# Sliding-window attention with sinks, followed by a maxout FFN: the order of the opening's instructions, chunks 0 to 3, written anew

## The chip, the cores and the metric

One Trainium2 chip, one of its cores. The metric is device time in microseconds (us), the median of the runs shown. The core has five engines that run their own instruction queues in order: TensorE (PE: matrix products, results to PSUM), VectorE (DVE), ScalarE (ACT), GpSimd (POOL) and SyncE (SP, which issues most transfers).

## What is computed

```python
scores = scale * np.matmul(q, k.transpose(0, 1, 3, 2))     # q, k, v: 4 x 8 x 768 x 64
keep = is_sink | in_window                                 # 4 sink keys, window of 128
scores = np.where(keep, scores, -1000000000.0)
scores = scores - np.max(scores, axis=-1, keepdims=True)
a = np.exp(scores)
a = a / (np.sum(a, axis=-1, keepdims=True) + 1e-09)
attn_out = np.matmul(a, v)
x = attn_out.transpose(0, 2, 1, 3).reshape(B * S, H * D)   # 3072 x 512
h = np.maximum(np.maximum(x @ w1, x @ w2), x @ w3)         # 3072 x 768
out = h @ w_out                                            # 3072 x 512
```

## The kernel before

**Tiling.** The 3072 tokens are 12 chunks of 256, three to a batch. A chunk's query rows see their own keys, the last 128 keys of the chunk before, and the four sinks of the batch (chunks 0, 3, 6 and 9 begin a batch and need neither). The eight heads are four pairs p. For each chunk c the kernel

- loads q, k and v (`load`, on SP's queue; a `gate` is a tiny write by GpSimd that the load has to wait for), casts them to bf16 (`cast_qk(c, w, g, engine)`, half g holding pairs 2g and 2g+1; `cast_v(c, n, i, engine)`, four quarters), and turns q and k with TensorE transposes and a copy out of PSUM (`turn`, L138 to L149; `turn2`), or by a transposing transfer (`turn_dma`);
- computes a pair's scores into two PSUM banks (`score`, L331). In chunks 0 and 1 the mask of some pairs is first put into the bank by a product (`premask`, L311); others are multiplied by a 0/1 mask after the exponential (`mask`, VectorE, L406). The masks are built by GpSimd and VectorE (`masks`, `factors`, `masks2`);
- takes the exponential on ScalarE, two halves to a pair (`expo`, L398), the sinks apart (`sink_k`, `sink_score`, `sink_v`);
- multiplies by the values, with a column of ones for the row sums (`av_open` takes four banks and adds the sinks' share; `av(c, p)`, L471), divides (`norm`, VectorE, L481 and L484) and turns the result to `xT` (`xpose`, L496 and L498, two halves; from chunk 3 on `xpose_dma`, one transfer);
- projects: `ffn_h(c, fp, wi)` is eight products with columns 256 fp to 256 fp + 255 of matrix wi (0, 1, 2 for w1, w2, w3) into one bank (L524), and `ffn_max` takes the bank into `h`: a copy for wi = 0 (L536, ScalarE unless told otherwise), a maximum for the others (L540, VectorE). With `then=False`, `av` and `ffn_h` leave `norm` and `ffn_max` to be written at another place. `ffn_y(c, t)` is half of the output product (L553, six products of 512 columns).

**The weights** come by GpSimd's queue in pieces (`load_w(wi, first column, last column)`, L292; `load_wo`).

**Order.** Nothing schedules: under `manual_schedule` each engine takes its instructions in the order in which the program's lines are written. The opening, chunks 0 to 3 with the attention of chunk 4, is one long list written out by hand, with the work of several chunks interleaved. From `for i in range(4, NCH)` a loop's body has one fixed order.

**PSUM.** Eight banks are handed out from a list, the one released longest ago first (`bank` and `give`). A write into a bank waits for what read it last, so the place of an `expo`, a `norm` or an `ffn_max` in the list sets when a later product can start.

`warm(n)` runs n products of zeros whose result nobody reads.

Of the kernel before, what the change touches and what calls it, by code (L numbers as in the profile page):

```python
# [999 lines left out]
```

## Time and profile before

| | us |
|---|---|
| median of 3 runs | 175.49 |
| lowest, highest | 175.13, 176.15 |
| the profiled execution's span, first to last instruction | 173.5 |
| TensorE busy in it | 167.7 |
| VectorE, GpSimd, ScalarE busy | 125.1, 110.1, 88.8 |

The profile is that of one execution. A timeline row gives an instruction's (or a run of equal instructions') start and length in us from the span's start, the engine, the line, what it writes and reads, and in brackets how long the engine stood idle before it and what ended that. A queue's name (POOLq, SPq) stands for the issuing of a transfer. Two equal instructions in a row overlap a little, so a run of them is shorter than the sum of their lengths.

### The profile page before, as it was taken

The numbers are of one execution on the slowest core, as the hardware profiler recorded it, in microseconds if no ns is written. First come the engines' busy times: TensorE is split into PE (matmuls) and PEld (weight loads), VectorE is DVE, ScalarE is ACT, GpSimd is POOL, SyncE is SP. The second block draws the span as 40 slices with busy tenths as digits, with TensorE's granted clock in tenths as the row PEclk, the third lists the DMA queues.
The fourth block names the chain that finished last, engine by engine and source line by source line (L and its number), as shares of the span: only waits on it lengthen the run. The fifth ranks groups of instructions, "written<-read, shape, count | busy, mean of one in ns | idle before, by whom it ended". The sixth has DMA issues, their size and how long they took to land.

```text
span 173.5 us, 5418 instructions
## 1 busy us (share of the span) xinstructions
PE 167.7 (97%) x2225; PEld 129.2 (74%) x2225; DVE 125.1 (72%) x262; ACT 88.8 (51%) x183; POOL 110.1 (63%) x193
## 2 busy tenths in 40 slices
PE   7979999999999999999999999999999999999992
PEld 2546889857695697797797797797897896896871
DVE  3187856696697985986877977877778876776361
ACT  4598554587944615817726717627636516510210
POOL 7389507445399999999999999999998700000000
PEclk9999999999999999999999999999999999999999
DMA  4999999999996999988999969969999119017303
GB/s 134 300 289 198 216 217 252 219 274 290 292 210 118 250 264 180 252 188 220 264 186 247 264 165 254 257 163 238 257 176 274 32 34 376 21 35 272 121 2 121
DMA packets 71545, 35.22 MB, mean 203 GB/s; under 512 B 27488, under 2 KB 69984, under 8 KB 71520
## 3 DMA queue, kind: packets, MB, share of 16 engines
q1 hardware_dynamic: 65824, 31.60, 79.0%
q0 software_dynamic: 5552, 3.15, 12.8%
q8 instruction: 17, 0.28, 0.7%
q10 hardware_dynamic: 144, 0.13, 0.2%
q14 instruction: 8, 0.07, 0.1%
HBM read 25.17 MB, written 6.29 MB: 181 GB/s over the span
## 4 chain that ended last, share of the span: by engine, by line
PE 93%; DVE 3%; ACT 1%; issue 0%
PE h_ps L524 55%; PE y_ps L577 11%; PE y_ps L553 7%; PE o L471 7%; PE st L357 3%; PE warm L203 3%; PE st L331 3%; PE pt L138 2%; ACT e_sb L398 1%; PE o L453 1%; DVE x_sb L484 1%; PE sk L423 1%; PE y_ps L599 1%; DVE vb L123 1%; PE xt L496 1%; PE st L311 0%
## 5 line engine op out<-in xcount | busy, mean ns | idle before, releaser
L524 PE MATMUL h_ps<-xT,w 128*128 128x256 bf16 x864 | 101.2, 273 | 0.1
L524 PEld LDWEIGHTS <-w 128*128 128x128 bf16 x864 | 81.9, 98 | 9.9 <-issue 0.3
L540 DVE TENSOR_TENSOR h_sb<-h_sb,h_ps 128x512 bf16<-128x512 bf16 (+1 forms) x74 | 49.3, 671 | 20.0 <-PE h_ps L524 16.0
L536 ACT CAST h_sb<-h_ps 128x512 bf16<-128x512 f32 x35 | 20.5, 585 | 52.2 <-PE h_ps L524 52.2
L129 POOL CAST vb<-v_raw 32x512 bf16<-32x512 f32 x48 | 36.7, 764 | 2.8 <-DMA v_raw<-in_v_dram 0.6
L90 POOL CAST k_bf<-k_raw 32x512 bf16<-32x512 f32 x48 | 29.5, 614 | 2.2
L398 ACT ACTIVATE e_sb<-st 128x512 bf16<-128x512 f32 (+1 forms) x48 | 23.1, 588 | 0.7 <-PE st L331 0.7
L484 DVE TENSOR_TENSOR x_sb<-o,rc 128x256 bf16<-128x256 f32 x48 | 20.4, 424 | 1.6
L577 PE MATMUL y_ps<-wo,h_sb 64*64 64x512 bf16 (+1 forms) x312 | 21.1, 377 | 0.0
L471 PE MATMUL o<-vb,e_sb 128*128 128x65 bf16 x352 | 16.8, 193 | 0.4 <-ACT e_sb L398 0.4
L471 PEld LDWEIGHTS <-e_sb 128*128 128x128 bf16 x352 | 14.6, 97 | 2.8 <-issue 0.8
L123 POOL CAST vb<-v_raw 64x512 bf16<-64x512 f32 x18 | 12.4, 691 | 5.8 <-DMA v_raw<-in_v_dram 5.2
L389 DVE TENSOR_TENSOR e_sb<-e_part,msk 128x1024 bf16<-128x1024 bf16 x16 | 13.5, 865 | 3.1 <-ACT e_part L374 3.0
L406 DVE TENSOR_TENSOR e_sb<-e_sb,msk 128x1024 bf16<-128x1024 bf16 (+1 forms) x18 | 13.3, 756 | 2.1 <-ACT e_sb L398 2.0
L577 PEld LDWEIGHTS <-h_sb 64*64 64x64 bf16 (+1 forms) x312 | 9.9, 106 | 5.0
L374 ACT ACTIVATE e_part<-st 128x384 bf16<-128x384 f32 x32 | 13.1, 496 | 0.5 <-PE st L357 0.5
L553 PE MATMUL y_ps<-wo,h_sb 128*128 128x512 bf16 x54 | 13.0, 380 | 0.0
L481 DVE RECIPROCAL rc<-o 128x4 f32<-128x4 f32 x48 | 8.3, 174 | 3.5 <-PE o L471 3.4
L118 POOL CAST k_bf<-k_raw 128x512 bf16<-128x512 f32 x6 | 3.8, 647 | 9.6 <-DMA k_raw<-in_k_dram 9.4
L553 PEld LDWEIGHTS <-h_sb 128*128 128x128 bf16 x54 | 4.8, 97 | 5.6 <-DVE h_sb L540 0.9
L118 ACT CAST q_bf<-q_raw 128x512 bf16<-128x512 f32 x13 | 7.6, 621 | 2.0 <-DMA q_raw<-in_q_dram 1.9
L427 ACT ACTIVATE e_sink<-sk 128x256 bf16<-128x256 f32 x8 | 3.1, 389 | 10.0 <-PE sk L423 10.0
(90 smaller groups left out, 144.2 us busy)
## 6 DMA issues: line engine op xcount, KB each, us to landing
k_raw<-in_k_dram SPq DMA_DIRECT2D x11, 512.0 KB, 5.7
v_raw<-in_v_dram SPq DMA_DIRECT2D x11, 512.0 KB, 5.8
q_raw<-in_q_dram SPq DMA_DIRECT2D x10, 512.0 KB, 6.5
out_dram<-y_sb SPq DMA_DIRECT2D x9, 512.0 KB, 3.1
w<-in_moe_w_dram POOLq DMA_DIRECT2D x9, 256.0 KB, 6.6
q_raw<-in_q_dram SPq DMA_DIRECT2D x4, 256.0 KB, 7.7
out_dram<-y_sb SPq DMA_DIRECT2D x1, 1024.0 KB, 5.2
wo<-in_moe_w_out_dram POOLq DMA_DIRECT2D x2, 384.0 KB, 7.4
```

The lines of the kernel that those rows point to most:

```text
L90: f(bfs[ci, "k"][x:x + 32, :, n], raws[ci, "k"][y:y + 32, :, i].rearrange("q (p a) d -> q p a d", a=2))
L123: eng.tensor_copy(vb[ci % RING][64 * i:64 * i + 64, n, :, 0:D], raws[ci, "v"][64 * n:64 * n + 64, :, i])
L129: eng.tensor_copy(vb[ci % RING][x:x + 32, n, :, 0:D], raws[ci, "v"][y:y + 32, :, i])
L389: nc.vector.tensor_mul(x.rearrange("q a (t s) c -> q (a t) s c", t=2), y, msk2)
L398: nc.scalar.activation(e[:, a, lo:], st[a][:, lo:], AF.Exp, scale=scale)
L471: nc.tensor.matmul(o[:, t, a], lhsT=e[:, a, s], rhs=vb[cv % RING][:, n, 2 * p + a], start=first, stop=True, skip_group_check=True)
L484: nc.vector.tensor_mul(xs[ci][:, p], o[:, :, :, 0:D], rc.unsqueeze(3).to_broadcast([128, 2, 2, D]))
L524: nc.tensor.matmul(hp[:, f].rearrange("q (i t r) -> q i t r", i=2, r=x.shape[3]), lhsT=w_sb[wi][:, ds, c0:c0 + 128], rhs=x, start=(ds == 0 ...
L536: (nc.scalar.copy if eng is nc.scalar else eng.tensor_copy)(dst, hp)
L540: nc.vector.tensor_max(dst[:, x], dst[:, x], hp[:, x])
L553: nc.tensor.matmul(yp, lhsT=hs[ci][:, fb, t * 128:(t + 1) * 128], rhs=wo[:, fb], start=(fb == 0), stop=(fb == FB - 1))
L577: nc.tensor.matmul(yps[ci][t][c:c + cols], lhsT=hs[ci][hp, fb, x:x + cols], rhs=wo[hp, fb], start=(turn == 0 and fb == 0), stop=(turn == 1 ...
```

## The change

Only the list of the opening is rewritten. The helper functions and the loop stay, and the computation is the same; one warm product of twelve goes.

- *Chunk 0:* `masks()` is written ahead of the casts, the mask products of two pairs ahead of the first turn, K is cast before Q, four of the warm products go behind the scores, and V's gate stands behind the masks on GpSimd.
- *Weights:* the first two pieces of w1 are issued before chunk 1's K cast; the last piece of w3 behind the cast of chunk 2's K.
- *Chunks 0 to 4:* every division and every maximum is now written apart from its products, most of them later. First copies (wi = 0) of some projections go from ScalarE to VectorE, three of the four V casts of chunk 5 from GpSimd to VectorE, the Q casts of chunk 4 from VectorE to ScalarE; `ffn_y(2, 1)`'s copy goes to ScalarE, `ffn_y(1, 1)`'s to VectorE.

The core of the difference:

```diff
         load(0, 'q', part=1, parts=2)
-        warm(8)
+        warm(7)
+        masks()
         load(0, 'k')
+        cast_qk(0, 'k', 1, nc.vector)
         load(0, 'q', part=0, parts=2)
         load(0, 'v', part=0, parts=2, gate=pool_gate)
-        cast_qk(0, 'q', 1, nc.scalar)
         load(0, 'v', part=1, parts=2)
-        masks()
         sink_init()
+        cast_qk(0, 'k', 0, nc.scalar)
+        premask(0, (2,))
+        cast_qk(0, 'q', 1, nc.gpsimd)
+        premask(0, (1,))
+        turn(0, 'q', 1, nc.vector)
+        turn(0, 'k', 1, nc.vector)
         factors(msk, addm)
-        turn(0, 'q', 1, nc.scalar)
+        cast_qk(0, 'q', 0, nc.vector)
+        turn(0, 'k', 0, nc.vector)
+        premask(0, (3,))
+        load(1, 'k')
+        cast_v(0, 1, 0, nc.gpsimd)
+        score(0, (2,))
+        expo(0, 2)
+        turn(0, 'q', 0, nc.vector)
+        score(0, (3,))
+        expo(0, 3)
+        cast_v(0, 0, 0, nc.vector)
+        premask(0, (0,))
+        load_w(0, 512, 768)
+        score(0, (0,))
+        load(1, 'q')
+        expo(0, 0)
+        score(0, (1,))
+        load(1, 'v')
+        cast_v(0, 1, 1, nc.vector)
         warm(4)
-        premask(0, (2,))
-        cast_qk(0, 'k', 0, nc.scalar)
-        cast_qk(0, 'k', 1, nc.vector)
-        turn(0, 'k', 1, nc.vector)
-        load(1, 'k')
-        turn(0, 'k', 0, nc.scalar)
-        cast_qk(0, 'q', 0, nc.gpsimd)
-        premask(0, (3,))
-        score(0, (2,))
-        score(0, (3,))
-        turn(0, 'q', 0, nc.vector)
-        premask(0, (0,))
-        load(1, 'q')
-        expo(0, 2)
-        cast_v(0, 1, 0, nc.gpsimd)
-        cast_v(0, 0, 0, nc.vector)
-        cast_v(0, 1, 1, nc.vector)
+        expo(0, 1)
         cast_v(0, 0, 1, nc.vector)
-        load_w(0, 512, 768)
-        load(1, 'v')
-        score(0, (0,))
-        expo(0, 3)
+        av_open(0)
+        av(0, 3, then=False)
+        norm(0, 3)
+        premask(1, (1,))
+        av(0, 2, then=False)
+        norm(0, 2)
+        premask(1, (0,))
+        av(0, 0, then=False)
+        load_w(0, 256, 512)
+        norm(0, 0)
+        cast_qk(1, 'k', 1, nc.scalar)
+        turn(1, 'k', 1, nc.vector)
+        av(0, 1, then=False)
+        norm(0, 1)
         cast_qk(1, 'k', 0, nc.gpsimd)
-        premask(0, (1,))
-        score(0, (1,))
-        expo(0, 0)
-        expo(0, 1)
-        load_w(0, 256, 512)
-        av_open(0)
-        av(0, 2)
-        av(0, 3)
-        turn2(1, 'k', 0, nc.vector)
...
         score(1, (0,))
+        expo(1, 0)
+        load_w(1, 256, 512)
         score(1, (1,))
-        expo(1, 0)
+        xpose(0, 1, nc.vector)
+        score(1, (3,))
+        expo(1, 3)
+        cast_v(1, 1, 1, nc.gpsimd)
+        sink_score(1)
+        load_w(1, 0, 256)
+        ffn_h(0, 2, 0, then=False)
+        ffn_max(0, 2, 0, 1, nc.vector)
+        score(1, (2,))
+        av_open(1)
+        cast_v(1, 1, 0, nc.gpsimd)
+        av(1, 0, then=False)
+        load(2, 'k', part=0, parts=2, gate=after(0, 300))
         expo(1, 1)
-        load_w(1, 256, 512)
-        cast_v(1, 1, 1, nc.gpsimd)
-        xpose(0, 1, nc.vector)
-        cast_v(1, 0, 1, nc.gpsimd)
-        load_w(1, 0, 256)
-        score(1, (3,))
-        sink_score(1)
-        load(2, 'k', part=0, parts=2, gate=after(0, 300))
+        av(1, 1, then=False)
+        ffn_h(0, 1, 0, then=False)
         load(2, 'k', part=1, parts=2)
-        sink_v(0)
-        expo(1, 3)
-        ffn_h(0, 2, 0, 1, nc.vector)
-        score(1, (2,))
-        load(2, 'q', part=1, parts=2)
         load(2, 'q', part=0, parts=2, gate=pool_gate)
+        expo(1, 2)
         load_w(2, 0, 256)
-        expo(1, 2)
+        mask(1, 3)
+        factors(msk0[0], addm0)
+        av(1, 3, then=False)
         load_w(2, 256, 512)
-        load_w(2, 512, 768)
-        av_open(1)
-        av(1, 0, then=False)
-        av(1, 1, then=False)
-        mask(1, 3)
-        ffn_h(0, 1, 0)
         norm(1, 0)
         mask(1, 2)
-        av(1, 3, then=False)
-        ffn_h(0, 0, 0)
+        ffn_h(0, 0, 0, then=False)
+        load(2, 'q', part=1, parts=2)
+        norm(1, 3)
+        av(1, 2, then=False)
+        norm(1, 1)
         load(2, 'v', gate=after(0, 300))
-        norm(1, 1)
-        av(1, 2, then=False)
-        norm(1, 3)
+        norm(1, 2)
...
+        ffn_h(1, 1, 0, then=False)
+        load_w(2, 512, 768)
+        ffn_h(0, 0, 1, then=False)
         load_wo()
-        factors(msk0[0], addm0)
-        ffn_h(1, 0, 1)
-        turn(2, 'k', 0, nc.vector)
+        ffn_max(0, 0, 0, 1, nc.vector)
         cast_v(2, 1, 0, nc.gpsimd)
+        ffn_max(1, 0, 0)
+        ffn_h(1, 1, 1, then=False)
+        ffn_max(1, 1, 0)
+        turn(2, 'k', 1, nc.scalar)
+        cast_qk(2, 'q', 0, nc.vector)
+        ffn_max(1, 1, 1)
+        ffn_max(1, 0, 1)
+        turn(2, 'q', 0, nc.scalar)
...
+        ffn_max(2, 0, 0, 1, nc.vector)
+        ffn_h(2, 1, 0, then=False)
+        ffn_h(2, 0, 1, then=False)
+        mask(3, 0)
+        ffn_max(2, 0, 2)
+        ffn_max(2, 1, 0)
+        mask(3, 3)
         score(3, (2,))
-        ffn_h(2, 0, 2)
-        mask(3, 0)
-        mask(3, 3)
-        ffn_h(2, 1, 0)
-        ffn_h(2, 0, 1)
         expo(3, 2)
         av_open(3)
+        ffn_max(2, 0, 1)
+        av(3, 1, then=False)
+        av(3, 0, then=False)
+        ffn_h(2, 2, 0, then=False)
+        sink_k(1)
+        ffn_h(2, 1, 1, then=False)
+        norm(3, 1)
+        av(3, 3, then=False)
+        cast_v(4, 1, 0, nc.gpsimd)
         mask(3, 2)
-        av(3, 0)
-        av(3, 1)
-        ffn_h(2, 1, 1, then=False)
-        av(3, 3)
-        ffn_h(2, 2, 0)
-        av(3, 2)
+        av(3, 2, then=False)
+        load(6, 'q')
+        ffn_h(2, 2, 1, then=False)
+        norm(3, 0)
+        cast_qk(5, 'k', 0, nc.gpsimd)
+        ffn_max(2, 2, 0)
+        norm(3, 3)
+        norm(3, 2)
+        cast_qk(5, 'k', 1, nc.scalar)
+        xpose_dma(3)
...
         cast_qk(5, 'q', 1, nc.gpsimd)
-        load(6, 'k')
-        turn_dma(5, 'q')
-        load(6, 'v')
-        masks2()
-        cast_v(5, 0, 0, nc.gpsimd)
-        cast_v(5, 0, 1, nc.gpsimd)
-        cast_v(5, 1, 0, nc.gpsimd)
-        cast_v(5, 1, 1, nc.gpsimd)
...
+        cast_qk(5, 'q', 0, nc.scalar)
+        expo(4, 3)
+        mask(4, 3)
+        load(6, 'k')
+        ffn_h(3, 1, 0, then=False)
+        cast_v(5, 1, 1, nc.vector)
+        ffn_h(3, 0, 0, then=False)
+        expo(4, 2)
+        mask(4, 2)
+        cast_v(5, 0, 0, nc.vector)
         mask(4, 1)
-        expo(4, 2)
-        ffn_y(2, 1, nc.vector)
-        mask(4, 2)
-        expo(4, 3)
-        ffn_h(3, 0, 0)
-        mask(4, 3)
-        ffn_h(3, 0, 1)
+        load(6, 'v')
+        ffn_h(3, 0, 1, then=False)
         av_open(4)
-        av(4, 0)
-        ffn_h(3, 0, 2)
-        av(4, 1)
-        ffn_h(3, 1, 0)
-        av(4, 2)
-        ffn_h(3, 1, 1)
-        av(4, 3)
+        ffn_max(3, 0, 0)
+        ffn_max(3, 0, 1)
+        ffn_h(3, 2, 1, then=False)
+        ffn_h(3, 1, 2, then=False)
+        cast_v(5, 0, 1, nc.vector)
+        av(4, 3, then=False)
+        norm(4, 3)
```

What this makes of three queues follows; the names in the rows carry buffer numbers, which differ between the two programs.

GpSimd's queue, from the V cast of chunk 0 (`vb0`) to the sinks of K; `w0` and `w1` are the matrices w1 and w2. Before:

```order
L123 CAST vb0_77<-v_raw_125 64x8x64
L292 DMA w0_107<-in_moe_w1_dram 128x4x256
L118 CAST k_bf_232<-k_raw_181 128x2x2x2x64
L292 DMA w0_107<-in_moe_w1_dram 128x4x256
L118 CAST q_bf_287<-q_raw_214 128x2x2x2x64
L292 DMA w0_107<-in_moe_w1_dram 128x4x256
L283 COPY ks0_81<-kT0_69 64x4x4 x2
```

And now:

```order
L123 CAST vb0_77<-v_raw_145 64x8x64
L292 DMA w0_107<-in_moe_w1_dram 128x4x256 x2
L118 CAST k_bf_285<-k_raw_190 128x2x2x2x64
L292 DMA w0_107<-in_moe_w1_dram 128x4x256
L118 CAST q_bf_310<-q_raw_224 128x2x2x2x64
L283 COPY ks0_81<-kT0_69 64x4x4 x2
L292 DMA w1_108<-in_moe_w2_dram 128x4x256 x2
```

Two transfers of w1 now stand ahead of chunk 1's K cast, and all three ahead of its Q cast; before, casts and transfers took turns.

ScalarE's queue, the exponentials of chunk 1. Before, `e_sb_343`, `350`, `373` and `416` are pairs 0, 1, 3 and 2:

```order
L398 ACTIVATE e_sb_343<-st_306 128x512
L398 ACTIVATE e_sb_343<-st_307 128x512
L398 ACTIVATE e_sb_350<-st_317 128x512
L398 ACTIVATE e_sb_350<-st_318 128x512
L427 ACTIVATE e_sink_379<-sk_374 128x256
L398 ACTIVATE e_sb_373<-st_365 128x512
L398 ACTIVATE e_sb_373<-st_366 128x512
L398 ACTIVATE e_sb_416<-st_408 128x512
L398 ACTIVATE e_sb_416<-st_409 128x512
```

Now `e_sb_352`, `377`, `362` and `408` are pairs 0, 3, 1 and 2:

```order
L398 ACTIVATE e_sb_352<-st_271 128x512
L398 ACTIVATE e_sb_352<-st_272 128x512
L398 ACTIVATE e_sb_377<-st_369 128x512
L398 ACTIVATE e_sb_377<-st_370 128x512
L427 ACTIVATE e_sink_386<-sk_381 128x256
L398 ACTIVATE e_sb_362<-st_258 128x512
L398 ACTIVATE e_sb_362<-st_259 128x512
L398 ACTIVATE e_sb_408<-st_400 128x512
L398 ACTIVATE e_sb_408<-st_401 128x512
```

Pair 3 and the sinks now come ahead of pair 1.

VectorE's queue in chunk 3: L406 are the masks of its four pairs, L540 and L536 the maxima and a first copy of chunk 2's projections, L481 and L484 divisions. Before, with pairs 1, 0, 3, 2:

```order
L406 TENSOR_TENSOR e_sb_929<-e_sb_929,msk0_0_101 128x2x384
L123 CAST vb3_80<-v_raw_732 64x8x64
L540 TENSOR_TENSOR h_sb_945<-h_sb_945,h_ps_979 128x512
L406 TENSOR_TENSOR e_sb_940<-e_sb_940,msk0_0_101 128x2x384
L406 TENSOR_TENSOR e_sb_964<-e_sb_964,msk0_0_101 128x2x384
L540 TENSOR_TENSOR h_sb_945<-h_sb_945,h_ps_1001 128x512
L406 TENSOR_TENSOR e_sb_978<-e_sb_978,msk0_0_101 128x2x384
L481 RECIPROCAL rc_1024<-o_1013 128x4
L484 TENSOR_TENSOR x_sb_1026<-o_1013,rc_1024 128x256
L481 RECIPROCAL rc_1034<-o_1014 128x4
L484 TENSOR_TENSOR x_sb_1026<-o_1014,rc_1034 128x256
```

Now, in the same order of the pairs except that the mask of pair 2, the last L406, comes later:

```order
L406 TENSOR_TENSOR e_sb_947<-e_sb_947,msk0_0_101 128x2x384
L536 CAST h_sb_950<-h_ps_960 128x512
L406 TENSOR_TENSOR e_sb_930<-e_sb_930,msk0_0_101 128x2x384
L540 TENSOR_TENSOR h_sb_950<-h_sb_950,h_ps_951 128x512
L406 TENSOR_TENSOR e_sb_940<-e_sb_940,msk0_0_101 128x2x384
L540 TENSOR_TENSOR h_sb_950<-h_sb_950,h_ps_989 128x512
L481 RECIPROCAL rc_1048<-o_1012 128x4
L484 TENSOR_TENSOR x_sb_1050<-o_1012,rc_1048 128x256
L406 TENSOR_TENSOR e_sb_1008<-e_sb_1008,msk0_0_101 128x2x384
L481 RECIPROCAL rc_1077<-o_1011 128x4
L484 TENSOR_TENSOR x_sb_1050<-o_1011,rc_1077 128x256
L481 RECIPROCAL rc_1083<-o_1014 128x4
```

The four masks are drawn apart; the one of pair 2 now stands behind three maxima or copies and pair 1's division.

More of the change, by code (lines that the diff above doesn't have):

```diff
@@ new lines @@
+        ffn_h(0, 0, 2, then=False)
+        ffn_max(1, 1, 2)
+        ffn_max(0, 0, 2)
+        ffn_h(0, 1, 2, then=False)
+        ffn_max(0, 1, 2)
+        cast_qk(2, 'q', 1, nc.scalar)
+        turn(2, 'q', 1, nc.scalar)
+        ffn_max(1, 2, 1)
+        ffn_h(1, 0, 2, then=False)
+        ffn_max(1, 0, 2)
+        score(2, (0,))
+        score(2, (3,))
+        expo(2, 0)
+        load(3, 'k')
+        score(2, (1,))
+        expo(2, 1)
+        sink_score(2)
+        mask(2, 0)
+        ffn_h(1, 2, 2, then=False)
@@ L801 @@
-        av(2, 2)
-        ffn_y(1, 0)
-        turn(3, 'k', 1, nc.scalar)
-        turn(3, 'k', 0, nc.scalar)
+        load(4, 'q', gate=after(0, 300))
+        score(2, (2,))
+        expo(2, 2)
+        load(4, 'k', gate=after(0))
+        ffn_y(0, 0)
+        cast_v(2, 0, 0, nc.vector)
+        mask(2, 3)
+        cast_qk(3, 'k', 1, nc.scalar)
+        mask(2, 1)
+        av_open(2)
+        mask(2, 2)
+        av(2, 0, then=False)
+        av(2, 3, then=False)
+        load(4, 'v')
+        ffn_y(0, 1)
@@ new lines @@
+        norm(2, 3)
+        cast_qk(3, 'q', 1, nc.vector)
+        cast_qk(3, 'q', 0, nc.gpsimd)
+        load(5, 'k', gate=after(0, 300))
+        cast_qk(3, 'k', 0, nc.vector)
+        av(2, 1, then=False)
+        load(5, 'q')
+        norm(2, 0)
+        ffn_y(1, 0)
+        av(2, 2, then=False)
+        turn(3, 'q', 1, nc.scalar)
+        turn(3, 'k', 0, nc.scalar)
+        cast_v(3, 0, 0, nc.gpsimd)
+        norm(2, 1)
+        norm(2, 2)
+        turn(3, 'k', 1, nc.vector)
+        turn(3, 'q', 0, nc.scalar)
@@ L805 @@
         xpose(2, 0, nc.scalar)
+        cast_qk(4, 'q', 1, nc.scalar)
         xpose(2, 1, nc.vector)
[L807 to L819 removed]
@@ new lines @@
+        cast_qk(4, 'k', 0, nc.gpsimd)
+        score(3, (3,))
+        score(3, (1,))
+        expo(3, 1)
+        ffn_h(2, 0, 2, then=False)
+        ffn_h(2, 0, 0, then=False)
+        cast_qk(4, 'k', 1, nc.vector)
+        turn_dma(4, 'k')
+        expo(3, 3)
+        expo(3, 0)
+        mask(3, 1)
+        cast_v(4, 1, 1, nc.gpsimd)
+        cast_v(3, 0, 1, nc.gpsimd)
+        ffn_max(2, 0, 0, 1, nc.vector)
+        ffn_h(2, 1, 0, then=False)
+        ffn_h(2, 0, 1, then=False)
+        mask(3, 0)
```

168 lines of the change are left out of this document (66 added, 102 removed).

## The prediction

> **What bounds the kernel now.** I read the page's engine shares and its chain first, then the windows by stage and TensorE's waits, and last the timelines of the first 70 us.
>
> ```profile
> PE 167.7 (97%) x2225; PEld 129.2 (74%) x2225; DVE 125.1 (72%) x262; ACT 88.8 (51%) x183; POOL 110.1 (63%) x193
> ...
> PE 93%; DVE 3%; ACT 1%; issue 0%
> ...
> 44.26:53.94 9.68, 9.68 (x114) 8.14 (x113) 8.39 (x19) 5.44 (x12) 7.06 (x13) 1.00 1.04 212
> 53.94:67.42 13.48, 13.48 (x162) 9.88 (x162) 10.79 (x22) 6.20 (x12) 12.62 (x27) 1.00 1.16 226
> 67.42:173.50 106.08, 102.72 (x1490) 82.01 (x1489) 77.17 (x148) 48.33 (x103) 65.14 (x97) 1.00 0.79 184
> ```
>
> TensorE is 97% busy, and the chain that ended last runs 93% on it. The window columns are length, then PE, PE loads, VectorE, ScalarE and GpSimd busy. From 15.88 us (the first projection) to 67.42 us (the loop's first instruction, the sink scores of chunk 5) TensorE has no idle time. The loop's own order is not edited. So the change is worth what it moves the loop's start, 67.42, as long as what the loop needs is there by then.
>
> ```profile
> PE pt L138 <- ACT k_bf L118: 0.3, 1, 0.3
> ...
> 1.26 3.60 PE L203 MATMUL warm<-wz 128*128 128x512 bf16 x8 [1.26 <-DVE wz L192]
> 5.08 1.67 PE L203 MATMUL warm<-wz 128*128 128x512 bf16 x4
> 7.81 0.50 PE L331 MATMUL st<-qT,kT 64*128 64x256 bf16 x8
> 10.64 0.53 PE L471 MATMUL o<-vb,e_sb 128*128 128x65 bf16 x12 [0.44 <-ACT e_sb L398]
> 15.88 1.03 PE L524 MATMUL h_ps<-xT,w 128*128 128x256 bf16 x8
> 21.70 5.40 PE L524 MATMUL h_ps<-xT,w 128*128 128x256 bf16 x48
> 36.34 2.76 PE L553 MATMUL y_ps<-wo,h_sb 128*128 128x512 bf16 x12
> 44.26 0.51 PE L331 MATMUL st<-qT,kT 64*128 64x256 bf16 x8
> 53.94 0.25 PE L437 MATMUL sv<-vb,sel 128*32 128x65 bf16 x8
> 67.42 0.29 PE L423 MATMUL sk<-qT,ks 128*32 128x256 bf16 x4
> ```
>
> These rows (start, length) give milestones at which old and new order have done the same set of TensorE work: 15.88 (first projection), 21.70 (chunk 1 attended and transposed), 36.34 (first output product), 44.26 (scores of chunk 3), 53.94 (sinks before chunk 4), 67.42. The 48 products in 5.40 give a projection's eight: 0.9, with no gap 0.87. TensorE's idle that the rows show after 7 us is some 1 us (0.28 and 0.44 the largest), so a gain has a low ceiling; a loss has none.
>
> **The change part by part.** The work is the same but for one warm matmul. I walk each queue by hand in its new order, with durations from rows, and compare at the milestones; a change in a bank's wait is read from the rule that the eight PSUM banks are reused in order of release.
>
> *Opening, to the first projection.*
>
> ```profile
> 5.78 0.43 DVE L118 CAST k_bf<-k_raw 128x512 bf16<-128x512 f32 x1 [1.91 <-DMA k_raw<-in_k_dram]
> 7.33 0.42 DVE L149 COPY kT<-pt 128x512 bf16<-128x512 bf16 x1 [1.13 <-PE pt L138]
> 8.19 3.17 ACT L398 ACTIVATE e_sb<-st 128x384 bf16<-128x384 f32 x8
> 9.03 1.47 DVE L123 CAST vb<-v_raw 64x512 bf16<-64x512 f32 x3
> 8.61 0.61 POOL L123 CAST vb<-v_raw 64x512 bf16<-64x512 f32 x1 [1.29 <-DMA v_raw<-in_v_dram]
> 9.17 1.11 POOL L292 DMA_DIRECT2D w<-in_moe_w_dram  x1
> 10.95 0.75 POOL L292 DMA_DIRECT2D w<-in_moe_w_dram  x1
> 12.12 0.61 POOL L118 CAST q_bf<-q_raw 128x512 bf16<-128x512 f32 x1 [0.43 <-DMA q_raw<-in_q_dram]
> ```
>
> The mask products of two pairs now fill the wait for K, and four warm matmuls go behind the scores. K's cast ends at 6.21 either way; the transposes follow at once, and the copy of kT ends at 7.15 instead of 7.75, so the first score starts at 7.2 instead of 7.81 and the eight exponentials (0.396 each) end 0.6 earlier, at 10.8. But the values need V's casts. V lands at 8.6 as before (its issue is gated some 0.5 later, behind the masks, in a stream that has earlier loads to finish); the three casts on VectorE now start on landing and end at 10.1, so the first values start at 10.15, not 10.64. Then GpSimd: two weight issues (1.11 and 0.75) stand ahead of chunk 1's K cast and a third ahead of its Q cast, which ends at 9.17 + 1.11 + 0.75 + 0.6 + 0.75 + 0.6 = 13.0 instead of 12.7. TensorE has by then, at about 12.5, nothing else in its order and waits 0.45. The two V casts of chunk 1 (0.5 each) stand on VectorE between the two copies of xT, so the second copy ends at 15.55 and the first projection starts at 15.65: **-0.23**. Ends: -0.6 (the early score kept whole) and +0.3 (a second issue at 1.11 too).
>
> *Chunk 1, 15.88 to 21.70.*
>
> ```profile
> 14.44 2.06 ACT L398 ACTIVATE e_sb<-st 128x512 bf16<-128x512 f32 x4
> 16.36 0.42 ACT L427 ACTIVATE e_sink<-sk 128x256 bf16<-128x256 f32 x1
> 16.62 2.12 ACT L398 ACTIVATE e_sb<-st 128x512 bf16<-128x512 f32 x4
> ```
>
> ScalarE's exponentials went pair 0, 1, sink, 3, 2 and now go 0, 3, sink, 1, 2, while the values go 0, 1, 3, 2. ScalarE starts at 14.65 (it copies qT at 14.1, after the late Q cast); at 0.515 each pair 1 is finished at 18.0, before at 16.5. The four sink products wait for the bank of the first projection, whose copy on VectorE ends at 17.4 (0.6 of wait), then pair 1's values wait from 17.85 to 18.05; behind them in TensorE's queue stand projections that are ready. Chunk 1 is transposed at 21.85 instead of 21.70: **+0.38** on top of the -0.23. Ends: 0 (pair 1 ready in time) and +1.0 (a whole pair's two exponentials exposed).
>
> *21.70 to 36.34.* VectorE's queue now has the cast of Q of chunk 2 ahead of eight maxima, and stands still until Q lands.
>
> ```profile
> 31.01 0.43 DVE L118 CAST q_bf<-q_raw 128x512 bf16<-128x512 f32 x1
> 29.13 0.62 ACT L118 CAST q_bf<-q_raw 128x512 bf16<-128x512 f32 x1
> 26.87 0.61 POOL L118 CAST k_bf<-k_raw 128x512 bf16<-128x512 f32 x1 [6.94 <-DMA k_raw<-in_k_dram]
> w<-in_moe_w_dram POOLq DMA_DIRECT2D x9, 256.0 KB, 6.6
> ```
>
> That half of Q is now issued before the other one, which before was cast at 29.13, and the last piece of w3 no longer goes ahead of it; I take 28.3 to 29.2. TensorE comes to its transposes at 29.26, so the wait is 0 to 0.4. The maxima then run 0.66 apart and free each bank before the projection that takes it. The last piece of w3 is issued behind chunk 2's K cast on GpSimd, at 26.6 to 27.4 by the row of 26.87, lands 6.6 later, 33.2 to 34.0, and is used at 34.4: hidden by 0.4 at the least. wo follows 0.75 later than that and just makes its use. The milestone comes at 36.45: **-0.04**. If Q landed only at 31.0 as in the old row, TensorE would wait 2.2; that is this term's other end.
>
> *36.34 to 67.42.*
>
> ```profile
> 45.67 0.84 POOL L118 CAST k_bf<-k_raw 128x512 bf16<-128x512 f32 x1 [1.71 <-DMA k_raw<-in_k_dram]
> 45.96 0.96 DVE L406 TENSOR_TENSOR e_sb<-e_sb,msk 128x768 bf16<-128x768 bf16 x1
> ...
> L406 DVE TENSOR_TENSOR e_sb<-e_sb,msk 128x1024 bf16<-128x1024 bf16 x10 | 6.8, 704 | 1.0 <-ACT e_sb L398 1.0
> ...
> L406 DVE TENSOR_TENSOR e_sb<-e_sb,msk 128x768 bf16<-128x768 bf16 x4 | 2.9, 754 | 0.0
> ...
> L484 DVE TENSOR_TENSOR x_sb<-o,rc 128x256 bf16<-128x256 f32 x48 | 20.4, 424 | 1.6
> ...
> L481 DVE RECIPROCAL rc<-o 128x4 f32<-128x4 f32 x48 | 8.3, 174 | 3.5 <-PE o L471 3.4
> ...
> 49.97 0.55 DVE L406 TENSOR_TENSOR e_sb<-e_sb,msk 128x768 bf16<-128x768 bf16 x1
> 52.62 2.66 DVE L540 TENSOR_TENSOR h_sb<-h_sb,h_ps 128x512 bf16<-128x512 bf16 x4
> xT<-x_sb SPq DMA_TRANSPOSE x9, 3.1
> ```
>
> Neighbours on VectorE overlap by some 0.05, so I count 0.65 for a mask of 1024, 0.66 for a maximum, 0.55 for a norm (0.174 + 0.424). To 44.26 one wait on a mask of chunk 2 (0.15) is all: **+0.13**. In chunk 3 VectorE goes on from 48.0 with mask, maximum, mask, maximum, norm, mask: 3 x 0.55 + 2 x 0.66 + 0.55 = 3.5, so pair 2's mask ends at 51.55; TensorE is at that pair's values at 51.2. **+0.22**. In chunk 4, VectorE takes three of the four V casts of chunk 5 that GpSimd did: from 59.05 mask, cast, mask, cast, mask, maximum (3 x 0.65 + 2 x 0.45 + 0.66) end at 62.6, and projection (3,1,1) takes that bank at 62.35; the next takes the bank of a norm that ends at 63.6. **+0.17**, and the loop starts at 68.05. The transfer of chunk 4's xT goes out then and lands 3.1 later, at 71.2; it is used 4.3 into the loop (72.4), so it stays hidden by 1.2. GpSimd has three casts less to do before the loop and costs nothing there.
>
> The walk used undisturbed durations. The mask of 0.96 beside the GpSimd cast of 0.84 shows the other price against 0.55. The two tight runs above have three masks each: 0 to 6 x 0.41 = 2.4. The old trace's four masks of this shape have a mean of 0.754, 0.2 over the low price, which makes 6 x 0.2 = 1.2; only the part that meets no other slack in its queue counts, and I take a third, **+0.4**.
>
> [...]
>
> Sum: -0.23 + 0.38 - 0.04 + 0.13 + 0.22 + 0.17 + 0.4 = **+1.0 us**. The profiled span is 173.5; the median 175.49 holds 2.0 more around it, which no part of this touches. Forecast: 175.5 + 1.0 = **176.5 us**.
>
> **The rivals.**
>
> *The early start is kept (faster).* Place: the first score, 0.6 earlier. Price: -0.6, and the waits of 0.44 and 0.28 on ScalarE in the old trace vanish, in all some -1.1: 174.4. It decides if chunk 1's Q cast comes by 12.5 and pair 1's exponentials by 17.4. For it: the new order places each bank's release shortly before its next use all through. Against it: the three weight issues on one queue.
>
> *VectorE becomes the bound from 44 to 67 us.* It is 19.2 of 23.1 us busy there (two window rows). The edit adds three casts (1.5) and the copies of two first maxima (2 x 0.66 = 1.3), 22.0 of 23.1; if these 2.8 are wholly exposed, in place of 0.22, 0.17 and 0.4 above, 176.5 + 2.0 = 178.5. Against it: one output copy goes to ScalarE.
>
> [...]
>
> *Nothing moves.* The reordered work lay under TensorE anyway and gains and waits cancel: 175.5.
>
> **How the numbers follow.** Forecast 0.47 (its own range 175.6 to 177.4), early start kept 0.24, VectorE as the bound 0.14, late clock 0.06, nothing 0.09. A change of less than 0.5% (0.9 us: 174.6 to 176.4) is about what a measurement of this kernel can't tell from none. Faster: 0.22, from the early start. Slower: 0.28 of the forecast with VectorE's and the clock's, 0.48. Same: the forecast's other 0.19, nothing moved, 0.09, and 0.02 of the early start, 0.30. The range reaches from 174.4 to 178.3: it leaves out about half of the early start's case (0.12) and half of VectorE's (0.07).
>
> **What would show it.** First score at about 7.2, first values at about 10.2; a TensorE wait on a GpSimd Q cast near 12.5 to 13; first projection within 0.3 of 15.65; waits on ScalarE or a bank at 17 to 18; waits on VectorE near 51 and 62; the loop's first sink score at 68 to 68.5. Wrong, if that sink score comes before 67.4 (then the opening's gain was kept, and the waits above are missing), if TensorE stands for 1 us or more near 29 (Q of chunk 2 late), or if the loop itself, from its first sink score to the end, is not 106 us long.

## The result and the profile after

The changed kernel takes 178.49 us (median of 5 runs, 178.22 to 178.52); the kernel before, on the same chip, 175.49 (5 runs). The ratio is 1.0162, 95% interval 1.014 to 1.0185: 3.0 us slower. The forecast was 176.5 with a range of 174.4 to 178.3, so the sign was right and the size too small, outside the range.

The page's engine shares and chain of the changed kernel:

```profile
PE 168.3 (95%) x2224; PEld 129.1 (73%) x2224; DVE 131.1 (74%) x273; ACT 86.6 (49%) x180; POOL 106.0 (60%) x185
...
PE 79%; DVE 7%; DMA 6%; POOL 3%; issue 2%; SPq 1%; POOLq 0%; DVEq 0%
```

The chain that ended last ran 93% on TensorE before. Now it is 79%, and 16% run over VectorE, transfers and GpSimd. The windows between the milestones of the prediction say where (columns: start and end, length, then busy PE, PE loads, VectorE, ScalarE, GpSimd, clock, DMA share, GB/s):

```profile
0.00:16.36 16.36, 13.35 (x134) 7.11 (x135) 11.05 (x35) 9.24 (x19) 12.45 (x33) 1.00 1.05 234
16.36:22.42 6.06, 5.77 (x87) 4.82 (x88) 4.85 (x12) 2.50 (x7) 3.81 (x8) 1.00 1.41 210
22.42:37.06 14.64, 14.64 (x160) 12.54 (x157) 9.18 (x17) 8.19 (x17) 4.51 (x10) 1.00 1.22 237
37.06:45.07 8.01, 8.01 (x93) 4.52 (x90) 7.09 (x19) 6.15 (x13) 3.77 (x4) 1.00 1.13 290
45.07:55.07 10.00, 9.85 (x113) 8.19 (x112) 9.23 (x20) 5.67 (x13) 7.69 (x17) 1.00 0.99 219
55.07:70.76 15.69, 13.97 (x161) 9.93 (x161) 12.67 (x25) 6.50 (x13) 13.15 (x25) 1.00 0.91 160
70.76:176.80 106.04, 102.71 (x1490) 81.97 (x1489) 77.04 (x149) 48.36 (x103) 60.58 (x91) 1.00 0.80 185
```

| stretch, to | before | after | difference | forecast |
|---|---|---|---|---|
| first projection | 15.88 | 16.36 | +0.48 | -0.23 |
| chunk 1 transposed | 5.82 | 6.06 | +0.24 | +0.38 |
| first output product | 14.64 | 14.64 | 0 | -0.04 |
| scores of chunk 3 | 7.92 | 8.01 | +0.09 | +0.13 |
| sinks ahead of chunk 4 | 9.68 | 10.00 | +0.32 | +0.22 |
| loop's first sink score | 13.48 | 15.69 | **+2.21** | +0.17, and part of +0.4 |
| end | 106.08 | 106.04 | 0 | 0 |

So 2.21 of the 3.3 us by which the span grew lie in one stretch, the attention of chunk 4 with the projections of chunk 3 (the *last stretch* from here on). In it the DMA share fell too, from 1.16 to 0.91. TensorE's rows that carry this, and the opening's:

```profile
7.07 0.34 PE L331 MATMUL st<-qT,kT 64*128 64x256 bf16 x4
10.16 0.34 PE L471 MATMUL o<-vb,e_sb 128*128 128x65 bf16 x6 [0.26 <-DVE vb L123]
13.12 0.40 PE L164 MATMUL pt<-ident,q_bf 128*128 128x128 bf16 x4 [0.40 <-POOL q_bf L118]
16.36 1.03 PE L524 MATMUL h_ps<-xT,w 128*128 128x256 bf16 x8 [0.76 <-DVE xT L498]
18.17 0.27 PE L453 MATMUL o<-vs,e_sink 32*128 32x130 bf16 x5 [0.29 <-DVE h_sb L536]
58.50 2.79 PE L524 MATMUL h_ps<-xT,w 128*128 128x256 bf16 x24 [0.53 <-DMA xT<-x_sb]
64.27 0.42 PE L471 MATMUL o<-vb,e_sb 128*128 128x65 bf16 x8 [0.65 <-DVE e_sb L406]
64.86 1.03 PE L524 MATMUL h_ps<-xT,w 128*128 128x256 bf16 x8 [0.18 <-DVE h_sb L540]
66.26 1.92 PE L524 MATMUL h_ps<-xT,w 128*128 128x256 bf16 x16 [0.36 <-DVE x_sb L484]
```

The last four rows hold 1.7 us of waits where the old order had none: 0.53 on the transfer of chunk 3's `xT`, then 1.19 in three waits on VectorE. The other 0.5 of the 2.21 is busy time (13.97 against 13.48). It fits the overlap of neighbours that each wait breaks, though nothing tests it: in the old trace the next products start 0.87 behind a projection's eight (60.49 and 61.36), which last 1.03. VectorE's rows for the masks of chunk 4, before:

```profile
57.02 1.49 DVE L406 TENSOR_TENSOR e_sb<-e_sb,msk 128x1024 bf16<-128x1024 bf16 x2
59.04 1.28 DVE L406 TENSOR_TENSOR e_sb<-e_sb,msk 128x1024 bf16<-128x1024 bf16 x2
```

and after, with the opening's two rows that matter:

```profile
14.41 1.48 DVE L123 CAST vb<-v_raw 64x512 bf16<-64x512 f32 x2
15.81 0.40 DVE L498 COPY xT<-xt 128x512 bf16<-128x512 bf16 x1
59.38 0.95 DVE L406 TENSOR_TENSOR e_sb<-e_sb,msk 128x1024 bf16<-128x1024 bf16 x1 [1.14 <-ACT e_sb L398]
61.42 0.43 DVE L123 CAST vb<-v_raw 64x512 bf16<-64x512 f32 x1 [1.09 <-DMA v_raw<-in_v_dram]
61.88 0.98 DVE L406 TENSOR_TENSOR e_sb<-e_sb,msk 128x1024 bf16<-128x1024 bf16 x1
62.79 0.83 DVE L123 CAST vb<-v_raw 64x512 bf16<-64x512 f32 x1
63.54 0.67 DVE L406 TENSOR_TENSOR e_sb<-e_sb,msk 128x1024 bf16<-128x1024 bf16 x1
```

At 60.33 VectorE comes to the first V cast of chunk 5 and stands 1.09, because V has not landed. Two masks of chunk 4 stand behind it. V is late since SP's queue is in another order. SP's issues (start, length, line, transfer) before:

```profile
52.77 1.24 SPq L503 DMA_TRANSPOSE xT<-x_sb  x1
54.10 0.53 SPq L107 DMA_DIRECT2D v_raw<-in_v_dram  x1
54.69 0.62 SPq L107 DMA_DIRECT2D q_raw<-in_q_dram  x1
```

and after:

```profile
51.91 0.57 SPq L107 DMA_DIRECT2D q_raw<-in_q_dram  x1
53.82 1.24 SPq L503 DMA_TRANSPOSE xT<-x_sb  x1
55.15 0.53 SPq L107 DMA_DIRECT2D v_raw<-in_v_dram  x1
```

The view of a tile's instructions gives the time from issue to landing, for this `xT` before

```profile
L503 SPq DMA_TRANSPOSE xT<-x_sb x1: 1240/1240/1240, 52.8 to 52.8; - x1
...
DMA to landing us min/median/max: 3.2/3.2/3.2
```

and after:

```profile
L503 SPq DMA_TRANSPOSE xT<-x_sb x1: 1238/1238/1238, 53.8 to 53.8; - x1
...
DMA to landing us min/median/max: 4.6/4.6/4.6
```

The diff moves `load(6, 'q')`, 512 KB, ahead of both. The transposing transfer takes 4.6 instead of 3.2, and V, by the same view of its tile, 6.2 instead of 5.2.

### The profile page after: what moved, and what is told of

It reads as the page before. It is cut to its first block, busy times and chain, and to the rows that moved or that the text cites. A ratio compares the mean times of both kernels' runs of the same rounds, so it can differ in the third digit from the quotient of the medians.

```text
span 176.8 us, 5419 instructions
## 1 busy us (share of the span) xinstructions
PE 168.3 (95%) x2224; PEld 129.1 (73%) x2224; DVE 131.1 (74%) x273; ACT 86.6 (49%) x180; POOL 106.0 (60%) x185
## 4 chain that ended last, share of the span: by engine, by line
PE 79%; DVE 7%; DMA 6%; POOL 3%; issue 2%; SPq 1%; POOLq 0%; DVEq 0%
PE h_ps L524 48%; PE y_ps L577 10%; DMA v_raw<-in_v_dram 6%; PE y_ps L553 6%; PE o L471 6%; PE st L357 3%; DVE vb L123 2%; DVE e_sb L406 2%; PE st L331 2%; POOL w L292 1%; DVE h_sb L540 1%; PE pt L138 1%; PE o L453 1%; DVE h_sb L536 1%; PE y_ps L599 1%
## 5 line engine op out<-in xcount | busy, mean ns | idle before, releaser
L540 DVE TENSOR_TENSOR h_sb<-h_sb,h_ps 128x512 bf16<-128x512 bf16 (+1 forms) x74 | 48.6, 669 | 15.3 <-PE h_ps L524 13.9
L536 ACT CAST h_sb<-h_ps 128x512 bf16<-128x512 f32 x31 | 18.0, 587 | 44.0 <-PE h_ps L524 43.0
L129 POOL CAST vb<-v_raw 32x512 bf16<-32x512 f32 x48 | 36.2, 755 | 3.5 <-DMA v_raw<-in_v_dram 1.3
L484 DVE TENSOR_TENSOR x_sb<-o,rc 128x256 bf16<-128x256 f32 x48 | 20.4, 424 | 1.6
L406 DVE TENSOR_TENSOR e_sb<-e_sb,msk 128x1024 bf16<-128x1024 bf16 (+1 forms) x18 | 13.3, 746 | 3.3 <-ACT e_sb L398 3.3
L389 DVE TENSOR_TENSOR e_sb<-e_part,msk 128x1024 bf16<-128x1024 bf16 x16 | 12.9, 817 | 3.4 <-ACT e_part L374 3.1
L123 POOL CAST vb<-v_raw 64x512 bf16<-64x512 f32 x13 | 8.9, 685 | 8.2 <-DMA v_raw<-in_v_dram 7.9
L374 ACT ACTIVATE e_part<-st 128x384 bf16<-128x384 f32 x32 | 13.1, 495 | 0.5 <-PE st L357 0.5
L553 PE MATMUL y_ps<-wo,h_sb 128*128 128x512 bf16 x54 | 13.1, 380 | 0.0
L481 DVE RECIPROCAL rc<-o 128x4 f32<-128x4 f32 x48 | 8.4, 174 | 3.7 <-PE o L471 3.4
L118 POOL CAST q_bf<-q_raw 128x512 bf16<-128x512 f32 x6 | 6.5, 1092 | 5.6 <-DMA q_raw<-in_q_dram 5.4
L118 ACT CAST q_bf<-q_raw 128x512 bf16<-128x512 f32 x15 | 8.8, 629 | 0.0
```

What stands on the lines that cost most here:

```text
L118: f(x[:, 2 * g:2 * g + 2].rearrange("q p i a d -> q p a i d"), y[:, 4 * g:4 * g + 4].rearrange("q (p a) i d -> q p a i d", a=2))
L129: eng.tensor_copy(vb[ci % RING][x:x + 32, n, :, 0:D], raws[ci, "v"][y:y + 32, :, i])
L406: (eng or nc.vector).tensor_mul(e[:, :, lo:], e[:, :, lo:], msk0[0] if lo else msk)
L484: nc.vector.tensor_mul(xs[ci][:, p], o[:, :, :, 0:D], rc.unsqueeze(3).to_broadcast([128, 2, 2, D]))
L536: (nc.scalar.copy if eng is nc.scalar else eng.tensor_copy)(dst, hp)
L540: nc.vector.tensor_max(dst[:, x], dst[:, x], hp[:, x])
```

## The experiments

Two edits are suspect in the last stretch: the queue order (Q of chunk 6 ahead of `xT`) and the V casts of chunk 5 on VectorE. The first runs take them out of the changed kernel one by one; the second group puts them into the kernel before; the rest goes to the opening. The last three columns come from each kernel's profile, one execution: the length of the last stretch, and the times from issue to landing of chunk 3's `xT` and chunk 5's V.

| kernel | median us | ratio to before, 95% | last stretch | xT | V |
|---|---|---|---|---|---|
| before | 175.49 | 1 | 13.48 | 3.2 | 5.2 |
| after | 178.49 | 1.0162 (1.014 to 1.0185) | 15.69 | 4.6 | 6.2 |
| after, V casts of chunk 5 on GpSimd | 177.18 | 1.0106 (1.0061 to 1.0152) | 15.03 | 5.7 | 6.1 |
| after, those casts on VectorE, later | 177.84 | 1.0139 (1.0098 to 1.018) | 14.17 | 4.8 | 6.4 |
| after, V of chunk 5 loaded first | 180.86 | 1.03 (1.0255 to 1.0345) | 16.59 | 7.1 | 4.5 |
| after, Q of chunk 6 behind xT and V | 177.39 | 1.01 (1.0061 to 1.0138) | 14.22 | 3.2 | 5.1 |
| after, both undone | 176.58 | 1.0044 (1.0013 to 1.0075) | 13.40 | 3.2 | 5.2 |
| the same, and V casts of chunk 1 behind xT | 176.29 | 1.0029 (0.9994 to 1.0063) | 13.71 | 3.3 | 5.2 |
| before, with Q of chunk 6 ahead of xT | 175.88 | 1.002 (0.9992 to 1.0048) | 13.84 | 5.7 | 6.2 |
| before, with the V casts on VectorE | 177.61 | 1.0123 (1.0078 to 1.0169) | 14.50 | 3.3 | 5.0 |
| before, with both | 179.51 | 1.0177 (1.008 to 1.0275) | 17.58 | 5.6 | 6.1 |
| after, V casts of chunk 1 behind xT | 178.88 | 1.0203 (1.0172 to 1.0235) | 16.06 | 6.3 | 5.9 |
| before, with the new chunk 0 | 175.98 | 1.0027 (0.9998 to 1.0055) | 13.45 | 3.5 | 5.2 |
| before, with the new opening to the first projection's copy | 177.18 | 1.0066 (1.0027 to 1.0105) | 13.57 | 3.2 | 5.2 |

**The V casts taken off VectorE.**

```diff
-        cast_v(5, 1, 1, nc.vector)
+        cast_v(5, 1, 1, nc.gpsimd)
```

and the same for `(5, 0, 0)` and `(5, 0, 1)`.

> The changed kernel with the three V casts of chunk 5 given back to GpSimd, at the same places of the list. Theory A (those casts stand on VectorE ahead of chunk 4's masks and wait there for V's landing, 1.09 us idle in the changed kernel's trace, and then take 0.4 to 0.8 each): VectorE's idle before the casts goes, the values of chunk 4 no longer wait for a mask (0.65) nor the next projections for banks (0.18, 0.36), the loop's first sink score comes at about 69.1 instead of 70.76, and the time is 178.5 - 1.7 = 176.8. Theory B (masks and maxima on VectorE are slowed by GpSimd's work beside them, wherever the casts stand): masks stay at 0.95, the sink score at 70.3 or later, 178.0 or more. Theory C (the late transfer of chunk 3's xT, 0.53 of wait, sets the lag): 178.5.

About 1.3 us come back by the medians. TensorE's waits on VectorE are gone. In the profile the stretch is still 1.5 too long, all of it a wait of 1.56 on `xT`: a second cause stands beside the first. That this wait is longer than the 0.53 of the changed kernel is not the edit's doing as far as the trace shows, for it comes ahead of the moved casts; the transfer took 5.7 here instead of 4.6.

**The same casts left on VectorE, but behind `ffn_max(3, 2, 2)`,** where V has long landed.

> The changed kernel with the same three V casts left on VectorE but written behind the last maximum of chunk 3, so that no mask, norm or maximum of chunks 3 and 4 stands behind them. Theory A, as a matter of place: as good as giving them back to GpSimd, 176.8, sink score at 69.1. If what counts is VectorE's load (2.0 us more of casts before the loop), the wait only moves into the loop's start and the time stays above 177.8. Theory C: 178.5.

The last stretch is 14.17, and 0.70 of that is a wait on `xT`; without it 13.47, the length before. But the median falls by 0.65 only, because the price has moved on into the loop, which lasts 106.95 instead of 106.04. VectorE casts there, and the masks of chunk 5 now stand behind the casts:

```profile
71.07 2.22 DVE L123 CAST vb<-v_raw 64x512 bf16<-64x512 f32 x3
73.32 3.01 DVE L406 TENSOR_TENSOR e_sb<-e_sb,msk 128x1024 bf16<-128x1024 bf16 x3
```

```profile
74.36 0.42 PE L471 MATMUL o<-vb,e_sb 128*128 128x65 bf16 x8 [0.46 <-DVE e_sb L406]
```

So the casts are not free on VectorE even where V has long landed; behind them, too, stands something that TensorE needs. (In this profile TensorE also waited 1.27 at 6.6 on the cast of chunk 0's K, which the changed kernel's profile does not have.)

**V of chunk 5 loaded earlier:** `load(5, 'v', gate=pool_gate)` moved ahead of `load(6, 'q')`.

> The changed kernel with the load of V of chunk 5 issued ahead of that of Q of chunk 6 and of chunk 3's xT, about 3 us earlier; the casts stay where they are on VectorE. If the wait for the landing (1.09) is what costs: VectorE's idle before the first cast goes, the time falls by 1.0 to 1.2, to 177.4. If the casts' own length and the contention with GpSimd cost (three casts took 1.95, two masks 0.95 and 0.98): at most 0.5 is won, 178.0 or more. A transfer more ahead of xT could make xT later than now (wait 0.53 to 1.0), which would take back up to 0.5.

The opposite of the gain expected: 2.4 us slower by the medians, 0.9 in the profile's stretch. The profiled run is the fastest of the four (179.58, mean granted clock 1.00); the other three took 180.8 to 181.1 at 0.99, so a part of the 2.4 may be TensorE's clock. TensorE's longest wait of the stretch:

```profile
61.29 2.79 PE L524 MATMUL h_ps<-xT,w 128*128 128x256 bf16 x24 [3.12 <-DMA xT<-x_sb]
```

V did come sooner (4.5), but now two loads stand ahead of the transposing transfer, and it takes 7.1. This was the run that put the queue order first among the causes.

**Q of chunk 6 put back behind them:** `load(6, 'q')` moved behind `load(5, 'v', ...)`, as it stands in the kernel before.

> The changed kernel with the load of Q of chunk 6 issued behind chunk 3's xT and V of chunk 5, as in the old order, instead of ahead of both; nothing else. Theory D (SP's queue: that 512 KB load, put ahead, holds back the transfer of xT, which took 4.6 us and more instead of 3.1, and then V of chunk 5, on which VectorE waits): xT lands some 3.2 after its issue, the wait of 0.53 goes, VectorE's idle of 1.09 shrinks to 0.5 or less, the loop's first sink score comes at 69.3 or earlier instead of 70.76, 177.0 or less. Theory A alone (VectorE's casts between the masks): xT's wait is beside the point, 178.0 or more.

`xT` lands after 3.2 again and TensorE no longer waits for it. The median falls by 1.1; of the stretch 14.22 is left against 13.48, with VectorE's casts as they were and no wait of theirs for V. The next run takes the casts out as well.

**Both undone.**

> The kernel of the run on the load of Q of chunk 6, with chunk 5's three V casts on GpSimd as well. If A and D are two waits of which each covers the other (with the casts moved alone, the wait for xT grew from 0.53 to 1.56): together they win more than either, the stretch from the sinks before chunk 4 to the loop is back at 13.6 or less instead of 15.7, sink score at 68.7, 176.4. If A was all, no more than the 177.2 of the casts alone.

```profile
55.32:68.72 13.40, 13.25 (x159) 9.88 (x160) 10.79 (x22) 6.40 (x13) 12.00 (x24) 1.00 1.02 217
```

The stretch is 13.40 long, and no wait of 0.15 or more is left in it. Together the two are worth 1.9 us by the medians; singly 1.1 and 1.3, as if each hid a part of the other.

**Each put alone into the kernel before, then both.** The edits are `load(6, 'q')` ahead of `xpose_dma(3)`, and the three casts on `nc.vector`, one ahead of each of `mask(4, 1)`, `mask(4, 2)`, `mask(4, 3)`.

> The kernel before, with only the load of Q of chunk 6 put ahead of chunk 3's transposing transfer of xT. Theory (queue order and V casts each cost about 1 us alone and more together): the transfer of xT takes 4.5 us or more instead of 3.2, TensorE waits 0.7 to 1.5 us before the projections of chunk 3, the loop's first sink score comes at 68.2 to 68.9, median 176.2 to 177.0. Rival (the queue order carries all of it): sink score at 70.5 or later, median 178.5 or more. Rival (harmless without the V casts on VectorE): sink score at 67.4, median 175.5.

> The kernel before, with only the three V casts of chunk 5 moved from GpSimd to VectorE, one ahead of each of chunk 4's masks 1, 2, 3. Theory (each about 1 us alone): V is cast on landing at 59.3 to 59.8, chunk 4's last mask comes 1.0 to 1.5 late, sink score at 68.2 to 68.9, median 176.2 to 177.0. Rival (the casts carry all of it): sink score at 70.5 or later, median 178.5 or more. Rival (harmless when V is on time): 67.4 to 67.7, median 175.5 to 175.8.

> The kernel before with only the two late edits put in: Q of chunk 6 loaded ahead of chunk 3's xT, and three V casts of chunk 5 on VectorE, one ahead of each of chunk 4's last three masks. If these two carry the loss of the last stretch wherever they stand: +1.5 to +3 on the kernel before, 177 to 178.5, with waits on xT or masks between 57 and 66. If the loss needs the lag that the new order has built up by then (1.1 at 54): under +0.5, 176.0 or less.

The queue order alone makes the transfer slow here too (5.7) and yet costs 0.36 in the stretch, in the median nothing that can be told from none:

```profile
58.44 1.92 PE L524 MATMUL h_ps<-xT,w 128*128 128x256 bf16 x16 [0.20 <-DMA xT<-x_sb]
```

The old order puts twelve output products between the scores of chunk 4 and the projections of chunk 3 and so comes to them 4.2 us after the sinks (53.94 to 58.16); the new one has six there and comes to them at 2.9 (55.07 to 57.97, the 58.50 of the row less its wait). The new order needs `xT` 1.3 us sooner and gets it later.

The casts alone lengthen the stretch by 1.02. The median grew by 2.1, but in that profile 1.5 us are lost ahead of the edited place, the largest part on a late K load of chunk 2, so the median can't be put down to the casts alone. With both edits the stretch is 4.1 longer in the profile. TensorE and VectorE there:

```profile
62.39 0.27 PE L453 MATMUL o<-vs,e_sink 32*128 32x130 bf16 x5 [2.07 <-DVE y_sb L555]
62.84 1.88 PE L524 MATMUL h_ps<-xT,w 128*128 128x256 bf16 x8
66.72 1.04 PE L524 MATMUL h_ps<-xT,w 128*128 128x256 bf16 x8
```

```profile
60.00 0.72 DVE L123 CAST vb<-v_raw 64x512 bf16<-64x512 f32 x1 [2.51 <-DMA v_raw<-in_v_dram]
60.75 0.98 DVE L406 TENSOR_TENSOR e_sb<-e_sb,msk 128x1024 bf16<-128x1024 bf16 x1
61.66 0.68 DVE L555 COPY y_sb<-y_ps 128x512 f32<-128x512 f32 x1
```

The cast waits 2.51 for a V that comes later, a mask and a copy stand behind it, and that copy gives free the bank that TensorE waits 2.07 for. One edit makes V late, the other puts VectorE's queue behind V. Not all of the 4.1 is that. TensorE is idle for 2.25, more than the 0.36 and 0.96 of the two edits alone; the other 1.85 is more busy time, and there the granted clock is low: 0.71 from 62 to 64 us, right behind the wait, 0.50 from 64 to 66 and 0.93 from 66 to 68, which is 1.7 us short of a clock of 1.00 in sum. A projection's eight products take 1.88 at 62.84, 1.67 at 64.97 and 1.04 at 66.72. Two of the four runs had a mean clock of 0.99 and two 1.00, the lowest (177.92) among these; how much of the median is the clock is open.

**The opening.** Chunk 1's two V casts moved behind the second copy of `xT`, `xpose(0, 1)`:

> The changed kernel with chunk 1's two V casts on VectorE written behind the second copy of xT of chunk 0 instead of ahead of it. Theory: these casts, 0.74 each in the changed kernel, hold the copy and by it the first projection (0.76 of wait). First projection at 15.65 instead of 16.36, time 178.5 - 0.7 = 177.8. Rival: the values of chunk 1 then wait for the casts, or the exponentials' order makes TensorE wait at 17 to 18.5 whatever comes before: milestone at chunk 1's transposes still 22.3 to 22.5, time 178.3 or more.

```profile
15.28 0.42 DVE L498 COPY xT<-xt 128x512 bf16<-128x512 bf16 x1 [0.71 <-PE xt L496]
15.73 0.95 DVE L123 CAST vb<-v_raw 64x512 bf16<-64x512 f32 x2
```

The first projection starts at 15.85 instead of 16.36 and the sinks ahead of chunk 4 come at 54.58 instead of 55.07: the 0.5 is carried on for 40 us. Then it is lost, and the median is 178.88.

```profile
59.82 2.79 PE L524 MATMUL h_ps<-xT,w 128*128 128x256 bf16 x24 [2.34 <-ACT e_sb L398]
```

The row names an exponential. But the changed kernel, with the same program here, starts these products at 58.50 while its exponentials run on to 60.33, so they do not need the last of them; what came just ahead is the transfer of `xT`, issued at 53.4 and landed 6.3 later, at 59.7. The same move with the last stretch mended:

> The same with chunk 1's two V casts behind the second copy of xT too. In the changed kernel this move brought the first projection 0.5 earlier and nothing at the loop's start, since xT of chunk 3 landed no earlier. Theory D: with that transfer out of the way the 0.5 is kept to the end, 175.9, sink score at 68.2. Rival (loads of chunks 3 to 5 arrive at the DMA's own pace, so that an earlier TensorE only waits there): 176.4 as without it.

First projection at 15.93, sinks ahead of chunk 4 at 54.71, 176.29 us. In the profile 0.3 of the 0.6 gained by the sinks is kept to the loop's start (68.42 against 68.72); the 0.3 between the medians is inside the intervals. What remains, 0.8 us by the medians, could be nothing: its interval against the kernel before holds 1.

Last, the new opening on top of the old order, cut after chunk 0 and after the first projection's copy (there with the V casts moved):

> The new order up to the last output scaling of chunk 0, then the order of before for all that is left. Theory (the opening's early start is real but spent on the wait for the Q cast behind the weight issues): first values at 10.2, a wait of about 0.4 on the GpSimd Q cast, first projection at 15.7 to 16.0, median 175.3 to 175.7. Rival (the early start is kept): first projection at 15.4, median 175.0 or less. Rival (what is left over in the run with all three parts mended sits in chunk 0): first projection at 16.3 or later, median 176.0 to 176.4.

> The new order up to the first projection's copy, with chunk 1's two V casts behind the second copy of xT, then the order of before for all that is left. Theory (the remaining 0.8 us of the run with all three parts mended comes from chunk 1's exponential order and from chunk 2 and 3): first projection at 15.9, chunk 1 transposed at 21.7 to 21.9, sink score at 67.4 to 67.7, median 175.4 to 175.8. Rival (it comes from the opening): sink score at 68.2 or later, median 176.2.

With chunk 0 alone: 175.98 us, ratio 1.0027 (0.9998 to 1.0055), and the first projection at 16.33, as the last rival had it. First values come early, at 10.31, but the old order then has TensorE wait 1.31 at 13.83 for a copy of chunk 1's K, so this cut is not the new order's own price. The longer cut: 177.18 us, ratio 1.0066 (1.0027 to 1.0105), but its 12 runs lie in two groups, five at 175.5 to 176.1 and seven at 177.1 to 177.8. First projection 15.86; the profile, of the upper group, loses 1.3 at 41.55 on a cast of chunk 3's Q behind a late V load of chunk 2. The lower group is close to the kernel before, which itself has five of 29 runs above 177. Why that load is late in some runs is not settled. No version was faster than the kernel before.

## Why the prediction fell short

- **Start of the opening: right.** First score 7.07 (7.2 forecast), first values 10.16 (10.15), a wait of 0.40 on GpSimd's Q cast at 13.1 (0.45 at 12.5).
- **First projection: a term of the sum mis-sized, +0.48 for -0.23.** The mechanism was named (the two V casts between the copies of `xT`), but the casts were taken at 0.5 each from a row of 1.47 for three. They took 0.74 each, with two weight issues and a V cast of GpSimd (14.87 to 15.60) beside them; behind the copy, in the experiment, with a weight issue (15.61 to 16.46) beside them, 0.95 for both. They also began at 14.41, some 0.25 later than the walk had it. The copy ended at 16.21, not 15.55.
- **Chunk 1: right in kind.** A bank wait at 17 to 18 (0.29), +0.24 for +0.38.
- **22 to 55 us: right.** 0, +0.09 and +0.32 for -0.04, +0.13 and +0.22.
- **A late clock, 0.06 of the chances: not seen.** The products around the first score take what they took before: eight transposes 0.62 at 6.15, against 0.61 for the same eight at 6.91, and four score products 0.34 at 7.07, against 0.34 at 9.16. The windows' clock can't tell this: it reads 1.00 from 0 to 4 us as well, where the warm products take 0.45 each; twelve output products of the same width take 2.76 at 36.34 before, 0.23 each. What makes the first ones slower no run shows.
- **Chunk 4: the step that failed, +2.21 for +0.17.** "From 59.05 mask, cast, mask, cast, mask, maximum" was walked as if V lay ready at 59. On VectorE's queue each cast was priced by its length, not by the arrival of its input; V landed at 61.4, and two masks stood behind it. And SP's queue was not walked there at all: the 512 KB load put ahead of `xT` and V, which makes the one 1.4 and the other 1.0 late, has no term in the sum. Both undone give the stretch back whole (13.40). What the sum left out is the wait for these two landings.
- **Contention, +0.4: right in kind, not the cause.** Masks of chunk 4 took 0.95 and 0.98 and a cast 0.83 beside a copy and casts of GpSimd, against 0.67 and 0.43 for others there. Those others overlapped GpSimd's casts too, and there GpSimd's grew: a V cast to 0.80 and two Q casts to 2.30 together, where the shortest of each in the trace takes 0.60. So in each of these pairs the one or the other grew. The time was not lost for that: the kernel with both edits undone still has three masks there in 2.69 (0.9 each) and loses nothing in the stretch, where three of the six masks stand that the prediction gave up to 2.4.
- **"VectorE becomes the bound", 178.5: the number of the result, for another reason.** VectorE was busy 21.9 us in the last two stretches (9.23 and 12.67), as forecast, but it stood idle 1.14 and 1.09 in the middle of the last one. That 178.5 came out is luck. With the load alone put back the stretch falls to 14.22, the casts still on VectorE. The casts are a real part of the price all the same: taking them off as well gives another 0.8, and written later they cost 0.9 in the loop. What no term of that rival holds is the load ahead of `xT` and V.
- **The loop: right,** 106.04 for 106.08. None of the three signs by which the prediction would have called itself wrong appeared; none of them asked whether the loop starts too late.

## What to carry to other kernels

An instruction moved into a queue that is taken in the written order can cost more than its length: here the first V cast took 0.43 and stood 1.09 for its input before that, and two masks of chunk 4 stood behind it. Ask of a moved load what it does to the transfers behind it: here one load put ahead made `xT` land after 4.6 instead of 3.2 and V after 6.2 instead of 5.2, so walk the DMA queue with the same care as the engines. Where two edits each look small, test them together too: in the kernel before the stretch grew by 0.36 and by 1.02 with one of them and by 4.1 with both, and there one made late what the other put VectorE's queue behind.
